# A recurrent mixer: loads and stores without the empty rows

## The chip, the cores and the metric

One Trainium2 chip, one core. The time is device microseconds of one execution; lower is better. Before the change three runs took 681.67, 686.21 and 689.05 us (median 686.21).

## The reference

Three stages, each over 4 batches and 768 time steps. First a recurrence in 8 heads of 40 x 40 state:

```python
for t in range(S):
    y[:, :, t] = einsum('bhd,bhde->bhe', rt, state)
    Sa = einsum('bhde,bhe->bhd', state, at)
    state = state * wt[:, :, None, :] - einsum('bhd,bhe->bhde', Sa, bt)
    state = state + einsum('bhd,bhe->bhde', vt, kt)
```

Then a gated convolution (five taps, a sigmoid, two 320 x 320 products) and a gated feed-forward part (320 to 1024, relu squared, back to 320, times a sigmoid gate). All values are float32.

## The kernel before

The recurrence is done in 24 chunks of 32 steps. A chunk's 32 pairs of batch and head lie as two halves of 16: 40 rows of the head dimension on partitions 0 to 39 for the even heads and 40 on partitions 64 to 103 (for v and r: 72 to 111) for the odd ones. The rows between the halves are empty; they hold zeros, or ones in w's columns.

For each chunk `plan_prep` loads `d` (w with its running product, then k, b and a; `load`, two transfers: columns 0 to 529 and the other 1536), runs a backward scan over w into `tl` (`bwd`, L181) and a forward scan into `ya` (`fwd`, L194), multiplies a by the forward scan (`ah`, L201) and k and b by the backward scan (`kbm`, L211), stores `ya` to DRAM (`yaout`), forms the small products of a with k and b (`gram`, L223, masked by `gmask`, L227) and transposes k and b (`ztr`, L236). `d`, `ya` are double-buffered. `plan_inv` inverts triangular 32 x 32 blocks on VectorE (L266, L267) for four chunks at a time. `plan_step` then does the recurrence between chunks: it loads v and r (`load_vr` into `vrt`), scanned rows from DRAM (`load_ys` into `ysj`, `load_wa` into `wa`) and multiplies v with r (`rv`, L359), the state with r (`yi`, L373) and so on (`gmm` L388, `umm` L400, `fmm` L420), ending with a new state. In `vrt` r stands in pairs of 32 columns, one of each pair zero in each half of the partitions, so that one matmul gives both halves' products side by side.

The two feed-forward stages (`Moe`) run beside this in 12 units of 64 steps. Their weights are split into two float32r parts on VectorE and ScalarE at the start (L683 to L699); L769, L821 and L829 are their matmuls.

All DMAs are issued by SyncE (SP) through `dma`, in one order. The order of all work is written out by hand: `ORDER` lists the tasks' numbers, and each engine and SP's queue get their instructions in that order. `BANKS` lists, in order of first use, which of four PSUM banks of its group a task's result goes to. A task that takes a bank waits until the bank's former user has been read. The numbers given to `add` beside an engine's letter (bytes and times of a DMA) do not reach the program.

Of the kernel before, what the change touches and what calls it, by code (L numbers as in the profile page):

```python
# [44 lines left out]
def mof(gr, i):  # L45
    return (i // 4) * 8 + gr * 4 + i % 4
# [49 lines left out]
class Attn:  # L96
    def __init__(self, ctx, tc, plan, fd, vr, vt, xs):
# [5 lines left out]
        psp = ctx.enter_context(tc.tile_pool(name="aps", bufs=1, space=PSUM))  # L103
        T = lambda name, shape: cp.tile(shape, F32, name=name)
        self.d = [T(f"d{i}", [PX, FDW]) for i in range(2)]
        self.ident = T("ident", [128, 128])
        make_identity(nc, self.ident)
        self.mask = T("mask", [128, L])
# [28 lines left out]
        self.s0 = [T(f"s0{i}", [PR, 8, D]) for i in range(2)]  # L137
        self.gs = [T(f"gs{i}", [128, 288]) for i in range(2)]
        self.ysj = T("ysj", [PX, NM, L + 1])
        self.ysb = T("ysb", [104, NM, 2 * L])  # L140
        self.vrt = [T(f"vrt{i}", [PR, 3 * NM * L]) for i in range(1)]
        self.tr = T("tr", [128, WCH, 8, L])
        self.sg, self.sz = T("sg", [128, WCH, 512]), T("sz", [128, 1, 640])
        self.pa = [psp.tile([128, 512], F32, name=f"pa{i}") for i in range(4)]
# [26 lines left out]

    def load(self, c, sl):
        self.dma(self.d[c % 2][:, sl], self.fd[c][:, sl])

    def kb(self, c):
        return self.d[c % 2][:, WL:WL + 1024]
# [34 lines left out]
        e.tensor_mul(kb, kb, t3.unsqueeze(2).to_broadcast([PX, 8, 2, L]))  # L211

    def yaout(self, c):
        self.dma(self.slya[c][0:PX], self.ya[c % 2])

    def gram(self, c, h):
        kb = self.kb(c).rearrange("p (m x) -> p m x", x=2 * L)
# [116 lines left out]
                 self.slz[c].rearrange("(x a) y -> a x y", x=2))  # L334

    def load_ys(self, c):
        self.dma(self.ysj.rearrange("p m l -> p (m l)"), self.slya[c][0:PX, 0:YS])

    def load_vr(self, c):
        self.dma(self.vrt[0], self.vr[c])  # L340

    def vpair(self, c, m):
        return self.vrt[0][:, m * L:m * L + L]

    def rpair(self, c, m):
        return self.vrt[0][:, NM * L + 2 * m * L:NM * L + 2 * m * L + 2 * L]

    def load_vt(self, c, gr):
        self.dma(self.mt[gr][64:96, :, 0:40], self.vt[c, gr])
# [5 lines left out]
    def rv(self, c):  # L355
        ps = self.bank("rv", c)
        for i in range(16):
            m, q, o = mof(i // 8, i % 8), i % 4, 2 * L * (i // 4)
            self.nc.tensor.matmul(ps[32 * q:32 * q + 32, o:o + 2 * L], lhsT=self.vpair(c, m), rhs=self.rpair(c, m),  # L359
                                  start=True, stop=True)  # L360

    def rvc(self, c):
# [6 lines left out]
    def yi(self, c, gr):  # L369
        s0, ps = self.s0[gr], self.bank("yi", c, gr)  # L370
        for i in range(8):
            r, o = i % 2 * 64, i // 2 * 2 * L
            self.nc.tensor.matmul(ps[r:r + 40, o:o + 2 * L], lhsT=s0[:, i, :], rhs=self.rpair(c, mof(gr, i)),  # L373
                                  start=True, stop=True)

    def yic(self, c, gr):
# [80 lines left out]
    def plan_prep(self, c):  # L457
# [3 lines left out]
        grams = [("gram", c - 2, h) for h in range(2)]  # L461
        add(("ldw", c), "d", [(1, 16, 7, 2120, 370)], lambda: self.load(c, slice(0, WL)),
            [("bwd", c - 2), ("fwd", c - 2)], p - 0.6)
        add(("ldk", c), "d", [(1, 16, 7, 6144, 370)], lambda: self.load(c, slice(WL, FDW)),
            grams + [("ah", c - 2)] + [("ztr", c - 2, k) for k in range(2)], p - 0.5)
        add(("bwd", c), "v", 1430, lambda: self.bwd(c),
            [("ldw", c), ("kbm", c - 1, 0), ("kbm", c - 1, 1), ("clc", c - 1), ("fwd", c - 1)], p)
# [5 lines left out]
        e = "v" if c < 3 else "g"  # L473
        for h in range(2):
            add(("kbm", c, h), e, 600 if e == "v" else 1250, lambda h=h: self.kbm(c, h, e), [("bwd", c), ("ldk", c)], p + 0.04)
        add(("yaout", c), "d", [(1, 16, 7, 4160, 380)], lambda: self.yaout(c), [("ah", c)], p + 0.3)
        for h in range(2):
            add(("gram", c, h), "p", 780, lambda h=h: self.gram(c, h),
                [("ah", c), ("kbm", c, h)], p + 0.1, bank=("a", "gram", c))
# [57 lines left out]
    def plan_step(self, c):  # L537
        P, add = self.plan, self.plan.add
        b = c + (HASTE[c] if c < len(HASTE) else 0.0)
        fs = lambda cc, g: [("fmm", cc, g, h) for h in range(2)]  # L540
        add(("lvr", c), "d", [(1, 16, 7, 6144, 370)], lambda: self.load_vr(c),
            [("rv", c - 1)] + [("yi", c - 1, g) for g in range(2)], b - 0.9)
        add(("lwa", c), "d", [(1, 10, 8, 2048, 370), (1, 16, 4, 2048, 370)], lambda: self.load_wa(c),
            [("yaout", c), ("stout", c, 0), ("gmm", c - 2, 0), ("gmm", c - 2, 1), ("fill", c % 2)], b - 0.8)
        add(("lzt", c), "d", [(1, 16, 8, 2560, 640)], lambda: self.load_zt(c),
            [("stout", c, 1), ("fill", 2 + c % 2)] + fs(c - 2, 0) + fs(c - 2, 1), b - 0.4)
        add(("lys", c), "d", [(1, 16, 7, 2112, 370)], lambda: self.load_ys(c),
            [("yaout", c)] + [("yb", c - 1, g, h) for g in range(2) for h in range(2)], b - 0.2)
        add(("rv", c), "p", 600, lambda: self.rv(c), [("lvr", c)], b - 0.1, bank=("a", "rv", c))
        add(("rvc", c), "a", 1520, lambda: self.rvc(c), [("rv", c)] + fs(c - 1, 0) + fs(c - 1, 1), b - 0.1,  # L550
# [408 lines left out]
def kernel(ctx, tc, fd, vr, vt, w_val, cw, w_out, mu, w_k, w_v, w_r, out, xs=None):  # L959
# [141 lines left out]
]  # L1101
BANKS = [
    "0123012301032201130320213031303230232231121313123100320122331231213220101230023102133111032203022303222121320132",
    "1023231231213012123123030232102103302101200313230203123130210310203321013202123012012032011032031203123010132101",
    "2301203123012313210123320122310031321202302203312031132003221332131223132313220210132103221032101220301202131232",
    "0310230303032011202302132130231033223132310230301123013231021323012012313030212330213101223012132323233223101221",
    "0323010321110320230321210211320301302112302132300231011301233120031213010120313122031130231031032313011023201130",
    "32232210321030231332013201",
]

# [1 line left out]
def arrays_of(inputs):  # L1112
    import numpy as np

    f = {k: np.ascontiguousarray(inputs[k]) for k in "rkvwab"}

    def fm(x):
        x = x.reshape(B, 4, 2, NCH, L, D).transpose(3, 2, 5, 1, 0, 4)
        return np.ascontiguousarray(x).reshape(NCH, 2, D, NM, L)

    def tm(x):
        x = x.reshape(B, 2, 2, 2, NCH, L, D).transpose(4, 5, 2, 1, 0, 3, 6)
        return np.ascontiguousarray(x.transpose(0, 2, 1, 3, 4, 5, 6)).reshape(NCH, 2, L, NM, D)
# [12 lines left out]
    fd = np.zeros((NCH, 128, FDW), np.float32)  # L1136
    f2 = fd.reshape(NCH, 2, 64, FDW)
    w = np.ones((NCH, 2, 64, NM, L + 1), np.float32)
    w[:, :, 0:D, :, 1:] = fm(f["w"])
    w[..., 0] = 0.0  # L1140
    f2[..., 0:YS] = w.reshape(NCH, 2, 64, YS)
    f2[:, :, 0:D, WL:WL + 1024] = np.stack([fm(f["k"]), fm(f["b"])], 4).reshape(NCH, 2, D, 1024)
    f2[:, :, 0:D, WL + 1024:] = fm(f["a"]).reshape(NCH, 2, D, 512)
    fd = np.ascontiguousarray(fd[:, 0:PX])
    vr = np.zeros((NCH, PR, 3 * NM * L), np.float32)
    r = np.zeros((NCH, PR, NM, 2, L), np.float32)
    for par in range(2):
        z = slice(72 * par, 72 * par + D)
        vr[:, z, 0:NM * L] = fm(f["v"])[:, par].reshape(NCH, D, NM * L)
        r[:, z, :, par] = fm(f["r"])[:, par]  # L1150
    vr[..., NM * L:] = r.reshape(NCH, PR, 2 * NM * L)
# [35 lines left out]
```

## Time and profile before

| | us or share |
|---|---|
| median of 3 runs | 686.21 |
| the profiled execution | 682.32 |
| its span | 680.3 |
| PE busy (matmuls) | 574.2, 84% |
| DVE busy | 525.3, 77% |
| ACT busy | 451.2, 66% |
| POOL busy | 236.9, 35% |
| SP's DMA queue | 116.75 MB, 66.2% of 16 DMA engines |

The busy times are averages over stages with different limits, so they are read by stretch, with the waits of each engine beside them. PE is TensorE, DVE VectorE, ACT ScalarE, POOL GpSimd; SPq is SyncE's queue, which issues the DMAs. L with a number is a line of the kernel. An engine's idle time counts only if somebody waits for that engine next.

### The profile page before, as it was taken

The page shows a single profiled execution, that of the slowest core. Times are in us where ns is not written, and L with a number is a line of the kernel's source. Part 1 is how long each engine was busy: PE and PEld are TensorE (multiplying, and loading weights), DVE is VectorE, ACT ScalarE, POOL GpSimd, SP SyncE. Part 2 cuts the span into 40 slices and gives each one's busy share as a digit, 9 for nine tenths or more (in the row PEclk, how much of TensorE's full clock was granted, in tenths as well). Part 3 has the DMA queues.
Part 4 walks back from the last instruction along what each step waited for, and adds up shares of the span by engine and source line. Part 5 has one row for each costly group of instructions (what it writes and reads, how often), then busy time and mean ns, then how long its engine had stood idle before and what let it go on. Part 6 is the DMA issues. An engine that isn't in the chain of part 4 may idle for free.

```text
span 680.3 us, 28916 instructions
## 1 busy us (share of the span) xinstructions
PE 574.2 (84%) x12368; PEld 519.3 (76%) x12368; DVE 525.3 (77%) x1236; ACT 451.2 (66%) x1153; POOL 236.9 (35%) x291
## 2 busy tenths in 40 slices
PE   2534367677889999999999898989999999999997
PEld 2433356566779978899888787979998989899897
DVE  9899878898878898889898876765898645545632
ACT  5545255355756767777686585768866889785843
POOL 1233223245153623446344423333313224151410
PEclk9999998566979999999999898999999999999999
DMA  8988989988877568876878835667527576332001
GB/s 250 266 266 280 256 232 225 267 217 260 218 196 161 170 196 227 250 158 180 273 202 137 206 87 149 166 167 148 150 68 163 132 176 171 83 84 74 1 20 40
DMA packets 137616, 118.59 MB, mean 174 GB/s; under 512 B 104208, under 2 KB 107280, under 8 KB 137488
## 3 DMA queue, kind: packets, MB, share of 16 engines
q1 hardware_dynamic: 137488, 116.75, 66.2%
q8 instruction: 97, 1.59, 1.1%
q14 instruction: 31, 0.25, 0.1%
HBM read 81.42 MB, written 35.30 MB: 172 GB/s over the span
## 4 chain that ended last, share of the span: by engine, by line
PE 59%; DVE 16%; ACT 7%; issue 6%; DMA 6%; POOL 1%; SPq 0%; DVEq 0%; POOLq 0%; ACTq 0%
PE pm L769 20%; PE pm L829 10%; PE pa L420 7%; PE pa L400 4%; PE pa L388 4%; PE pm L821 3%; PE pa L443 3%; PE pa L223 3%; PE pa L373 2%; DVE pm L949 2%; DMA d<-in_fd_dram 2%; PE pa L236 2%; DVE mt L429 2%; DVE tmv L266 2%; DVE tn L267 2%
## 5 line engine op out<-in xcount | busy, mean ns | idle before, releaser
L412 POOL TENSOR_TENSOR mt<-mt,mask 64x512 f32<-64x512 f32 x48 | 65.5, 1367 | 207.1 <-ACT mt L407 184.6
L407 ACT COPY mt<-pa 32x288 f32<-32x288 f32 x192 | 74.7, 389 | 16.3 <-PE pa L400 13.7
L769 PE MATMUL pm<-hh,whk 128*128 128x256 f32 x288 | 82.8, 296 | 1.4 <-ACT hh L739 0.9
L769 PE MATMUL pm<-hh,wlk 128*128 128x256 f32 x288 | 79.6, 285 | 0.0
L949 DVE SCALAR_TENSOR_TENSOR pm<-X,cw,pm 128x256 f32<-128x256 f32 (+1 forms) x144 | 67.0, 482 | 13.3 <-ACT pm L947 10.8
L420 PE MATMUL pa<-mt,zt 128*40 128x72 f32 x1536 | 63.5, 239 | 11.6 <-issue 5.2
L267 DVE TENSOR_TENSOR tn<-tn,tmv 128x31 f32<-128x31 f32 (+15 forms) x155 | 66.2, 427 | 5.3
L266 DVE TENSOR_TENSOR tmv<-tn,al 128x31 f32<-128x31 f32 (+15 forms) x155 | 62.9, 406 | 8.0 <-POOL tn L261 3.7
L420 PEld LDWEIGHTS pa<-mt,zt 128*40 128x40 f32 x1536 | 54.6, 124 | 18.5 <-issue 8.0
L429 DVE TENSOR_TENSOR mt<-pa,cl 40x160 f32<-40x160 f32 x184 | 58.5, 318 | 10.4 <-PE pa L420 8.5
L211 POOL TENSOR_TENSOR d<-d,tl 112x512 f32<-112x512 f32 x42 | 51.5, 1237 | 38.9 <-DVE tl L181 16.1
L829 PE MATMUL pm<-whv,kh 128*128 128x320 f32 x192 | 62.7, 326 | 0.0
L223 PE MATMUL pa<-ya,d 40*32 40x32 f32 x3072 | 42.8, 216 | 23.5 <-issue 10.5
L223 PEld LDWEIGHTS pa<-ya,d 40*32 40x32 f32 x3072 | 37.6, 128 | 30.3 <-issue 14.8
L829 PE MATMUL pm<-wlv,kh 128*128 128x320 f32 x192 | 59.5, 310 | 1.3 <-issue 1.3
L829 PE MATMUL pm<-whv,kl 128*128 128x320 f32 x192 | 59.5, 310 | 0.0
L769 PEld LDWEIGHTS pm<-hh,whk 128*128 128x128 f32 x288 | 55.6, 193 | 4.1 <-ACT hh L739 1.0
L236 PE MATMUL pa<-ident,d 104*128 104x104 f32 x192 | 35.8, 331 | 24.8 <-DVE d L211 11.8
L769 PEld LDWEIGHTS pm<-hh,wlk 128*128 128x128 f32 x288 | 55.7, 193 | 0.0
L769 PE MATMUL pm<-hl,whk 128*128 128x256 f32 x192 | 55.2, 288 | 0.4 <-POOL hl L744 0.4
L814 DVE TENSOR_TENSOR kl<-pm,kh 128x512 fp32r<-128x512 f32 x48 | 32.4, 686 | 28.1 <-ACT kh L812 27.9
L236 PEld LDWEIGHTS pa<-ident,d 104*128 104x128 f32 x192 | 25.3, 182 | 30.0 <-issue 11.0
(138 smaller groups left out, 1606.8 us busy)
## 6 DMA issues: line engine op xcount, KB each, us to landing
d<-in_fd_dram SPq DMA_DIRECT2D x24, 672.0 KB
vrt<-in_vr_dram SPq DMA_DIRECT2D x24, 672.0 KB
slya<-ya SPq DMA_DIRECT2D x24, 455.0 KB
slz<-sz SPq DMA_DIRECT2D x24, 320.0 KB
zt<-slz SPq DMA_DIRECT2D x24, 320.0 KB
d<-in_fd_dram SPq DMA_DIRECT2D x24, 231.9 KB
ysj<-slya SPq DMA_DIRECT2D x24, 231.0 KB
slg<-sg SPq DMA_DIRECT2D x20, 256.0 KB
```

Source lines behind the costliest of these rows:

```text
L211: e.tensor_mul(kb, kb, t3.unsqueeze(2).to_broadcast([PX, 8, 2, L]))
L223: self.nc.tensor.matmul(ps[p:p + L, m * L:(m + 1) * L], lhsT=kb[r:r + 40, m, o:o + L], rhs=ah[r:r + 40, m, :], start=True, stop=True)
L236: self.nc.tensor.transpose(ps[:, 128 * i:128 * i + 104], self.kb(c)[0:104, o:o + 128], self.ident[0:104, 0:104])
L266: v.tensor_mul(t3, tn[:, 0:h, k:k + 1].to_broadcast([128, h, nt]), al[:, k:k + 1, k + 1:n].to_broadcast([128, h, nt]))
L267: v.tensor_add(tn[:, 0:h, k + 1:n], tn[:, 0:h, k + 1:n], t3)
L407: self.nc.scalar.copy(self.mv(gr)[96:128, 4 * mh:4 * mh + 4, par, :], ps[32 * q:32 * q + 32, 0:288].rearrange("p (m x) -> p m x", x=72))
L412: self.nc.gpsimd.tensor_mul(mm, mm, self.mask[64:128].unsqueeze(1).to_broadcast([64, 16, L]))
L420: self.nc.tensor.matmul(ps[r:r + 40, k * 72:k * 72 + 72], lhsT=self.zt[c % 2][:, zof(mof(gr, i)) + par, :], rhs=self.mt[gr][:, 2 * i + par ...
L429: self.nc.vector.tensor_mul(self.mv(gr)[0:40, 4 * mh:4 * mh + 4, par, 0:40], p3[r:r + 40, :, 0:40], cn[r:r + 40, m0:m0 + 4].unsqueeze(2).t ...
L769: self.nc.tensor.matmul(ps[0:n, (mt % 2) * NT:(mt % 2) * NT + NT], lhsT=ww[:, mt * 128:mt * 128 + n], rhs=xx, start=(i == 0), stop=(i == l ...
L829: self.nc.tensor.matmul(ps[:, 0:DM], lhsT=xx[:, k, sl], rhs=ww, start=(k == 0 and i == 0), stop=(k == 7 and i == 2))
L949: self.nc.vector.scalar_tensor_tensor(o, X[0:n, k, :, t:t + TW], self.cw[0:n, k, t:t + 1], o, ALU.mult, ALU.add)
```

## The change

The rows between the halves are no longer moved. k, b and a are loaded in two transfers of 48 rows (partitions 0 to 47 and 64 to 111) in place of one of 112; w's columns are loaded as before. The scanned rows are stored and loaded back in two times 48 rows. v and r are packed anew: `vrt` is three layers of 16 x 32 columns, and each half of the partitions gets two layers (r and v on partitions 0 to 47 in layers 0 and 1; v and r on partitions 64 to 111 in layers 1 and 2), so that the zero partner of r in each half is a layer that no transfer writes. r's pair of 32 columns is then layer 0 and layer 2, two runs of 32 columns. What no transfer writes is filled with zeros once at the start: `d` on VectorE, `ysj` and `vrt` on GpSimd. `ORDER` is unchanged; `BANKS` names other banks in some places, 168 of 586. The figures in `add` change, and the host packs v and r anew.

```diff
         self.d = [T(f"d{i}", [PX, FDW]) for i in range(2)]
+        for t in self.d:
+            nc.vector.memset(t[32:64, WL:], 0.0)
...
         self.ysj = T("ysj", [PX, NM, L + 1])
+        nc.gpsimd.memset(self.ysj[32:64], 0.0)
...
-        self.vrt = [T(f"vrt{i}", [PR, 3 * NM * L]) for i in range(1)]
+        self.vrt = T("vrt", [PR, 3, NM, L])
+        nc.gpsimd.memset(self.vrt, 0.0)
...
+    def load_k(self, c):
+        for r in (0, 64):
+            self.dma(self.d[c % 2][r:r + 48, WL:], self.fd[c][r:r + 48, WL:])
...
     def yaout(self, c):
-        self.dma(self.slya[c][0:PX], self.ya[c % 2])
+        for r in (0, 64):
+            self.dma(self.slya[c][r:r + 48], self.ya[c % 2][r:r + 48])
...
     def load_ys(self, c):
-        self.dma(self.ysj.rearrange("p m l -> p (m l)"), self.slya[c][0:PX, 0:YS])
+        for r in (0, 64):
+            self.dma(self.ysj[r:r + 48].rearrange("p m l -> p (m l)"), self.slya[c][r:r + 48, 0:YS])
 
     def load_vr(self, c):
-        self.dma(self.vrt[0], self.vr[c])
+        for i in range(2):
+            self.dma(self.vrt[64 * i:64 * i + 48, i:i + 2].rearrange("p z m l -> p (z m l)"), self.vr[c, i])
 
     def vpair(self, c, m):
-        return self.vrt[0][:, m * L:m * L + L]
+        return self.vrt[:, 1, m]
 
     def rpair(self, c, m):
-        return self.vrt[0][:, NM * L + 2 * m * L:NM * L + 2 * m * L + 2 * L]
+        return self.vrt[:, 0:3:2, m]
...
-            self.nc.tensor.matmul(ps[32 * q:32 * q + 32, o:o + 2 * L], lhsT=self.vpair(c, m), rhs=self.rpair(c, m),
+            self.nc.tensor.matmul(self.two(ps[32 * q:32 * q + 32, o:o + 2 * L]), lhsT=self.vpair(c, m), rhs=self.rpair(c, m),
                                   start=True, stop=True)
...
-        add(("ldk", c), "d", [(1, 16, 7, 6144, 370)], lambda: self.load(c, slice(WL, FDW)),
+        add(("ldk", c), "d", [(2, 16, 3, 6144, 370)], lambda: self.load_k(c),
...
 BANKS = [
-    "0123012301032201130320213031303230232231121313123100320122331231213220101230023102133111032203022303222121320132",
+    "0123012301032201130320213031303230232231121313123100320122331231213220101232003120133111230003200323002121302130",
```

VectorE's first instructions of before, from the start of the program (`rst`, `seed`, `xj` are constants, `pa` the PSUM banks, `tl` the first backward scan):

```order
L118 MEMSET rst 112x530
L119 MEMSET rst 112x17
L122 MEMSET seed 112x528
L129 MEMSET xj 128x256
L146 MEMSET pa_130 128x512
L146 MEMSET pa_131 128x512
L146 MEMSET pa_132 128x512
L146 MEMSET pa_133 128x512
L848 MEMSET X 128x12x4
L181 SCALAR_TENSOR_TENSOR tl<-d_68,rst 112x529
```

The same of the changed kernel:

```order
L107 MEMSET d_68 32x1536
L107 MEMSET d_69 32x1536
L120 MEMSET rst 112x530
L121 MEMSET rst 112x17
L124 MEMSET seed 112x528
L131 MEMSET xj 128x256
L150 MEMSET pa_134 128x512
L150 MEMSET pa_135 128x512
L150 MEMSET pa_136 128x512
L150 MEMSET pa_137 128x512
L863 MEMSET X 128x12x4
L189 SCALAR_TENSOR_TENSOR tl<-d_68,rst 112x529
```

The two fills of `d` stand ahead of all that was there.

SP's first DMAs of before, with what each waits for (DMAHW0 to DMAHW7 are eight counters that the DMAs use in turn; DVE, PE and so on are engines):

```order
L156 DMA d_68<-in_fd_dram 112x530
L643 DMA buf<-in_cw_dram 128x30
L156 DMA d_68<-in_fd_dram 112x1536
L156 DMA d_69<-in_fd_dram 112x530
L643 DMA wt<-in_w_val_dram 64x640 x2
L156 DMA mt<-in_vt_dram 32x16x40
L643 DMA buf<-in_w_val_dram 128x640
L643 DMA wt<-in_w_val_dram 128x640 [waits DMAHW0_49]
L643 DMA mu<-in_mu_dram 128x6 [waits DMAHW1_49]
L156 DMA d_69<-in_fd_dram 112x1536 [waits DMAHW2_49]
L156 DMA slya_186<-ya_104 112x1040 [waits DMAHW3_49,DVE_49]
```

The same of the changed kernel:

```order
L160 DMA d_68<-in_fd_dram 112x530
L658 DMA buf<-in_cw_dram 128x30
L160 DMA d_68<-in_fd_dram 48x1536 [waits DVE_49]
L160 DMA d_68<-in_fd_dram 48x1536
L160 DMA d_69<-in_fd_dram 112x530
L658 DMA wt<-in_w_val_dram 64x640 x2
L160 DMA mt<-in_vt_dram 32x16x40
L658 DMA buf<-in_w_val_dram 128x640 [waits DMAHW0_49]
L658 DMA wt<-in_w_val_dram 128x640 [waits DMAHW1_49]
L658 DMA mu<-in_mu_dram 128x6 [waits DMAHW2_49]
L160 DMA d_69<-in_fd_dram 48x1536 [waits DMAHW3_49,DVE_49]
L160 DMA d_69<-in_fd_dram 48x1536 [waits DMAHW4_49]
```

The k load of the first chunk is a pair, and the first of the pair waits for VectorE's fill; from the ninth DMA on each waits for the eighth before it, which with the pairs is a later piece of work than it was.

## Rows read from the trace of the kernel before

**Rows 1.** Busy us by stretch: span, each engine (instructions), PEclk, DMA share, GB/s

```profile
0.00:60.00 60.00, 22.59 (x857) 19.08 (x858) 56.05 (x111) 31.71 (x71) 14.71 (x24) 1.00 0.93 272
60.00:120.00 60.00, 34.93 (x1206) 29.48 (x1209) 50.66 (x121) 27.90 (x79) 18.36 (x16) 0.95 0.93 234
120.00:200.00 80.00, 59.97 (x1524) 51.73 (x1513) 71.12 (x166) 43.96 (x116) 30.64 (x30) 0.67 0.87 239
200.00:440.00 240.00, 226.61 (x4852) 204.63 (x4851) 201.03 (x474) 169.78 (x440) 103.04 (x122) 0.99 0.71 181
440.00:681.00 241.00, 230.07 (x3953) 214.36 (x3951) 146.40 (x368) 177.87 (x449) 70.13 (x99) 1.00 0.44 107
```

**Rows 2.** DVE's waits, 0 to 200 us: releaser, us in total, times, longest

```profile
DVE pm L689 <- DMA buf<-in_w_v_dram: 1.6, 2, 1.2
DVE tmv L266 <- DMA al<-slg: 1.2, 1, 1.2
...
DVE pm L689 <- DMA buf<-in_w_out_dram: 0.6, 1, 0.6
...
DVE tl L181 <- DMA d<-in_fd_dram: 0.4, 1, 0.4
```

**Rows 3.** Waits of POOL and PE that DMAs ended, whole trace

```profile
POOL d L211 <- DMA d<-in_fd_dram: 15.5, 4, 9.7
...
PE pa L359 <- DMA vrt<-in_vr_dram: 0.3, 1, 0.3
```

**Rows 4.** SP's DMA queue (packets, MB, share) and issues (KB each)

```profile
q1 hardware_dynamic: 137488, 116.75, 66.2%
...
d<-in_fd_dram SPq DMA_DIRECT2D x24, 672.0 KB
vrt<-in_vr_dram SPq DMA_DIRECT2D x24, 672.0 KB
```

**Rows 5.** DVE's timeline at the start: start us, us, line, operation

```profile
0.98 0.50 DVE L118 MEMSET rst<- 112x530 f32 x1 [0.98 <-PEq L1174]
...
2.56 2.11 DVE L146 MEMSET pa<- 128x512 f32 x4
4.64 1.22 DVE L181 TENSOR_TENSOR_SCAN tl<-d,rst 112x529 f32<-112x529 f32 x1
```

**Rows 6.** DVE's timeline at 18 us, the idle time before in brackets

```profile
18.07 1.26 DVE L181 TENSOR_TENSOR_SCAN tl<-d,rst 112x529 f32<-112x529 f32 x1 [0.82 <-ACT cl L190]
```

**Rows 7.** POOL's timeline at the start

```profile
2.62 0.95 POOL L260 MEMSET tn<- 128x1024 f32 x1
...
21.31 1.47 POOL L201 TENSOR_TENSOR ya<-d,ya 112x512 f32<-112x512 f32 x1 [17.53 <-DVE ya L194]
```

**Rows 8.** SP's issues by tile: ns min/median/max, first and last start

```profile
L156 SPq DMA_DIRECT2D d<-in_fd_dram x48: 312/408/2520, 0.8 to 411.6; - x48
...
L156 SPq DMA_DIRECT2D vrt<-in_vr_dram x24: 322/424/1717, 33.8 to 594.5; - x24
...
L156 SPq DMA_DIRECT2D slya<-ya x24: 303/380/1637, 9.3 to 439.2; - x24
...
L156 SPq DMA_DIRECT2D ysj<-slya x24: 304/549/2416, 51.2 to 612.9; - x24
```

**Rows 9.** SP's waits: us in total, times, longest

```profile
SPq L156 <- PE pa L420: 49.1, 18, 11.1
...
SPq L156 <- DMA d<-in_fd_dram: 10.2, 9, 2.7
```

**Rows 10.** PE's groups by form: out<-in, shapes, count, busy us, mean ns

```profile
L373 PE MATMUL pa<-vrt,s 112*40 112x64 f32 x736 | 28.8, 226 | 2.0 <-ACT s L446 1.9
L359 PE MATMUL pa<-vrt 112*32 112x64 f32 x768 | 16.9, 227 | 4.5 <-issue 2.7 <-DVE ysb L436 0.6 <-ACT s L446 0.5
```

**Rows 11.** Timelines of DVE and PE at 117 us

```profile
117.18 0.68 DVE L227 TENSOR_TENSOR sg<-pa,gm 128x512 f32<-128x512 f32 x1
...
117.37 1.18 PE L373 MATMUL pa<-vrt,s 112*40 112x64 f32 x16
```

More of the change, by code (lines that the diff above doesn't have):

```diff
@@ L336, in load_ys, with two @@
     def load_ys(self, c):
-        self.dma(self.ysj.rearrange("p m l -> p (m l)"), self.slya[c][0:PX, 0:YS])
+        for r in (0, 64):
+            self.dma(self.ysj[r:r + 48].rearrange("p m l -> p (m l)"), self.slya[c][r:r + 48, 0:YS])
     def load_vr(self, c):
-        self.dma(self.vrt[0], self.vr[c])
+        for i in range(2):
+            self.dma(self.vrt[64 * i:64 * i + 48, i:i + 2].rearrange("p z m l -> p (z m l)"), self.vr[c, i])
     def vpair(self, c, m):
-        return self.vrt[0][:, m * L:m * L + L]
+        return self.vrt[:, 1, m]
     def rpair(self, c, m):
-        return self.vrt[0][:, NM * L + 2 * m * L:NM * L + 2 * m * L + 2 * L]
+        return self.vrt[:, 0:3:2, m]
+    @staticmethod
+    def two(ps):
+        return ps.rearrange("p (r l) -> p r l", l=L)
     def load_vt(self, c, gr):
@@ L372, in yi @@
             r, o = i % 2 * 64, i // 2 * 2 * L
-            self.nc.tensor.matmul(ps[r:r + 40, o:o + 2 * L], lhsT=s0[:, i, :], rhs=self.rpair(c, mof(gr, i)),
+            self.nc.tensor.matmul(self.two(ps[r:r + 40, o:o + 2 * L]), lhsT=s0[:, i, :], rhs=self.rpair(c, mof(gr, i)),
                                   start=True, stop=True)
@@ L475, in plan_prep @@
             add(("kbm", c, h), e, 600 if e == "v" else 1250, lambda h=h: self.kbm(c, h, e), [("bwd", c), ("ldk", c)], p + 0.04)
-        add(("yaout", c), "d", [(1, 16, 7, 4160, 380)], lambda: self.yaout(c), [("ah", c)], p + 0.3)
+        add(("yaout", c), "d", [(2, 16, 3, 4160, 380)], lambda: self.yaout(c), [("ah", c)], p + 0.3)
         for h in range(2):
@@ L540, in plan_step @@
         fs = lambda cc, g: [("fmm", cc, g, h) for h in range(2)]
-        add(("lvr", c), "d", [(1, 16, 7, 6144, 370)], lambda: self.load_vr(c),
+        add(("lvr", c), "d", [(2, 16, 3, 4096, 370)], lambda: self.load_vr(c),
             [("rv", c - 1)] + [("yi", c - 1, g) for g in range(2)], b - 0.9)
@@ L546, in plan_step @@
             [("stout", c, 1), ("fill", 2 + c % 2)] + fs(c - 2, 0) + fs(c - 2, 1), b - 0.4)
-        add(("lys", c), "d", [(1, 16, 7, 2112, 370)], lambda: self.load_ys(c),
+        add(("lys", c), "d", [(2, 16, 3, 2112, 370)], lambda: self.load_ys(c),
             [("yaout", c)] + [("yb", c - 1, g, h) for g in range(2) for h in range(2)], b - 0.2)
@@ L1102 @@
 BANKS = [
-    "0123012301032201130320213031303230232231121313123100320122331231213220101230023102133111032203022303222121320132",
[L1104 to L1107, printed above, removed]
+    "0123012301032201130320213031303230232231121313123100320122331231213220101232003120133111230003200323002121302130",
+    "1023031031013010123103230230120103320101220313030023123132012310023301213022103210210230211030231023103210130101",
+    "0321003123210313010123302120312031301020320203310231130203021330131203130313022012130123021230121202301022131032",
+    "2310032323030211022300130132031033203130310232301103213031221303210210313032012332013101203210130303033203121201",
+    "2303012301112320032301012011302301320110320132302031211321233100231013210102313120231132031231232313211023021130",
     "32232210321030231332013201",
@@ L1144, in arrays_of @@
     fd = np.ascontiguousarray(fd[:, 0:PX])
-    vr = np.zeros((NCH, PR, 3 * NM * L), np.float32)
-    r = np.zeros((NCH, PR, NM, 2, L), np.float32)
+    vr = np.zeros((NCH, 2, 48, 2 * NM * L), np.float32)
     for par in range(2):
[L1148 to L1151, printed above, removed]
+        z = slice(8 * par, 8 * par + D)
+        vr[:, par, z, NM * L * (1 - par):NM * L * (2 - par)] = fm(f["v"])[:, par].reshape(NCH, D, NM * L)
+        vr[:, par, z, NM * L * par:NM * L * (par + 1)] = fm(f["r"])[:, par].reshape(NCH, D, NM * L)
     a = {"fd": fd, "vr": vr,
```

## The prediction, made before the changed kernel ran

> **What bounds the kernel now.** I read the busy time by stretch first [rows 1]. There are two kernels in one. Up to 200 us VectorE (DVE) is busy 56.05 of 60, 50.66 of 60 and 71.12 of 80 us, together 177.8 of 200; TensorE (PE) is busy 117.5. From 200 us to the end PE is busy 456.7 of 481 us, and DVE falls to 347. The DMA engines are nearly full early (0.93, 0.93, 0.87) and have room later (0.71, 0.44). So a full DMA share and a full DVE stand side by side in the first 200 us, and the question is which of them the other waits for. For that I read who ended DVE's waits in the first 200 us [rows 2]: DMA rows add up to 1.6 + 1.2 + 0.6 + 0.4 = 3.8 us, of which only the 0.4 us belongs to a tile that the change touches (the scan's wait on d, and that on its unchanged columns). The 15.5 us that POOL waited on loads of d in the whole trace [rows 3] are idle time of an engine that is busy only 33.1 of the first 120 us [rows 1]. So DVE paces the early part and PE the late part; the loads arrive mostly in time.
>
> **The change part by part.**
>
> Bytes. For each of 24 chunks the k/b/a load goes from 112 to 96 rows of 6144 B (98,304 B less), the scanned rows' store from 112 to 96 rows of 4160 B (66,560 B), their load back from 112 to 96 of 2112 B (33,792 B), and v with r from 112 x 6144 B to 96 x 4096 B (294,912 B). The two largest sizes of before are in [rows 4]. That is 493,568 B a chunk, 11.85 MB in all, 10.1% of the queue's 116.75 MB. The queue's packets took 66.2% of 680.3 us, so about 45 us of time of all 16 DMA engines goes. What that is worth is set by the waits that DMAs end, not by the 45 us. On DVE up to 200 us these are 3.8 us [rows 2]; a tenth fewer bytes takes at least a tenth of them, 0.4 us, and at most all, 3.8 us. A nearly full queue gets shorter by more than its bytes, so I take half: **-1.9 us** (bounds -0.4 and -3.8). After 200 us PE has 24.3 us of idle time in 481 us [rows 1]; PE's own wait on v and r is 0.3 us in the whole trace [rows 3], so I add nothing there.
>
> Two new zero fills on DVE. They are the first instructions of its program, 32 x 1536 each. The trace has DVE fills of 112 x 530 in 0.50 us and of 128 x 512, four in 2.11 us [rows 5], 0.94 to 1.03 ns for a column. 1536 columns are 1.45 to 1.58 us, two of them 2.9 us. In before, DVE ran from 0.98 to 4.67 us through such fills and started the first scan without a wait, at 4.64 [rows 5]; the load of w for it had landed. So the whole 2.9 us goes ahead of the first scan, and everything that DVE does in the first 60 us (idle there 3.95 us, 0.98 of it before its first instruction) stands behind it. The first cover is the scan at 18.07 us, which waited 0.82 us for ACT's copy of the totals [rows 6]: ACT is not moved by the fills up to that point, so 0.8 us is absorbed. **+2.1 us** is left (bounds 0 and +2.9: nothing if later waits swallow it all). The first k load also waits now for the fill of d0, at about 0.98 + 1.45 = 2.4 us where it was issued at 1.72 before; k and b are multiplied only after both first scans, which end later by the same 2.9 us, so this is covered.
>
> Two new zero fills on POOL, 112 x 1536 and 32 x 528. POOL's fill of 128 x 1024 took 0.95 us [rows 7], so these are about 1.4 and 0.5 us. Behind them POOL has nothing that anyone wants soon: it sat idle 17.5 us until 21.31 [rows 7]. **0.**
>
> Split transfers. Each of the four becomes two issues, 96 more on SP's one queue. The medians of an issue are 408 ns (d), 424 (vrt), 380 (slya) and 549 (ysj) [rows 8]; 24 x (0.408 + 0.424 + 0.380 + 0.549) = 42 us of SP time. What hides it is that SP waits for others: for PE L420 alone 49.1 us [rows 9]. The second half matters only where a load ends somebody's wait on the path, and then by one issue, 0.4 us, against a transfer that is shorter. Of DVE's and PE's waits above, none or one is of that kind. **+0.3 us** (bounds 0 and +42). The order also shows that every DMA waits for the eighth one before it (the names DMAHW0 to 7 go round). With pairs the eighth one before is a more recent one; SP's waits that ended with a landing of d were 10.2 us in 9 cases [rows 9]. While the queue is full its engines have work anyway, so I count this at 0, and keep it as a rival.
>
> [...] First the row: a second issue costs 0.38 to 0.55 us of SP, and the rows beside it show no price for the transfer itself being cut in two. [...]
>
> Matmuls with v and r. Their moving operand, 112 x 64 before in one run, is now two runs of 32 with a gap. Nothing in this trace has that form. 736 matmuls of the state with r fill 28.8 us, 768 of v with r 16.9 us [rows 10]. If the two runs cost nothing, 0; if each such matmul took twice its share, +45.7 us. The nearest rows are these same matmuls, with as many columns and rows, and only the place of half of the columns differs; I take **0**.
>
> PSUM banks. 168 of the 586 bank uses get another bank; the order of work is the same. I followed both strings through the program and, for each use, asked in the trace of before whether the bank's previous user was done when the use begins. With the new string this fails once: the state-times-r matmuls at 117.37 now take the bank that DVE L227 reads until 117.18 + 0.68 = 117.86 [rows 11]. **+0.5 us** (bounds 0 and +3, since ends and starts move).
>
> The sum: 2.1 - 1.9 + 0.3 + 0.5 = **+1.0 us**. The profiled execution took 682.3 us (680.3 of span and 2.0 around it), so its like would take 683.3. That execution is near the lowest of the three timed runs (681.67, 686.21, 689.05); against their median of 686.21 I forecast **687.2 us**, no change that can be measured: a difference under 1%, 6.9 us, can't be told from none here.
>
> **The rivals.**
>
> DMA paces the early part after all. For it: shares of 0.93, 0.93 and 0.87 mean 181 us of work of all engines in the first 200 us [rows 1]. Then 10.1% of that, 18 us, goes, and with the fills 2.1 us come back: 686.2 - 18 + 2.1, about 670 us. Against it: 3.8 us of DVE waits. Half of this gain, 678 us, is where it would first be told from nothing.
>
> The queue of issues becomes the bound (slower). Place: SP, in the stretches where it issues one DMA right after another. Price: the step's two loads, v with r and the scanned rows, each 24 times, 24 x (0.424 + 0.549) = 23 us, giving about 710 us; with all four, 42 us and 728. It decides from the point where SP has the next issue ready and nothing to wait for; 17 of the 96 extra issues on the path are 6.9 us. Against it: SP's waits for engines [rows 9]. [...]
>
> The two-run operand costs (slower). At twice the share 686 + 45.7, 732 us; even a sixth more would pass 1%. Nothing in the trace speaks for it.
>
> [...]
>
> **How the numbers follow.** No change, as summed: 0.57, with a range of its own from 680 to 693. DMA paces: 0.18. Issues bound: 0.12. Two-run operand: 0.04. Clock: 0.09, split about evenly, 0.04 faster and 0.05 slower. So faster by over 1% 0.22, within 1% 0.57, slower by over 1% 0.21. For 8 in 10 the range must take in the nearer halves of the rivals on both sides: from 675 (beyond it the better half of the DMA case, 0.09) to 699 (beyond it most of the issue case and the operand, about 0.11).
>
> **What would show it.** Right: DVE's first scan at about 7.5 us in place of 4.64 and the scan of 18.07 at about 20.2; about 105 MB on the queue and a DMA share of about 0.6; PE's matmuls of v and r at a mean of 226 ns as before; PE busy about 457 us after 200 us, and DVE about as busy as before in the first 200. Wrong: DVE work that ends well before 200 us while DVE's idle time there falls by more than 4 us (the DMA case); SP's waits that end with a landing much over 10 us, and waits of PE or POOL on vrt or ysj (the issue case); longer rows for v and r (the operand); another clock in 100 to 200 us.

## The result, and the profile after

The changed kernel takes 673.21 us (median of 4 runs, 672.54 to 675.11) against 685.46 (4 runs, 681.67 to 689.05): a ratio of 0.985 with a 95% interval from 0.981 to 0.990. It is 1.5% faster, 14 us below the forecast of 687.2 and just below the forecast's range (675 to 699). The ratios here and below leave out executions in a slower state of the chip, the medians do not, so the two can differ by some tenths of a percent.

Busy time by stretch of the changed kernel (columns as in [rows 1], the last stretch ends with the span of 671.2 us):

```profile
0.00:60.00 60.00, 22.76 (x869) 19.22 (x872) 57.39 (x111) 31.00 (x70) 17.36 (x26) 1.00 0.92 243
60.00:120.00 60.00, 36.45 (x1158) 30.75 (x1152) 50.89 (x122) 28.16 (x79) 18.33 (x16) 1.00 0.94 225
120.00:200.00 80.00, 59.92 (x1565) 51.83 (x1564) 69.03 (x161) 44.33 (x118) 30.62 (x30) 0.96 0.82 202
200.00:440.00 240.00, 229.39 (x5164) 208.15 (x5163) 212.09 (x502) 177.45 (x459) 107.29 (x126) 1.00 0.73 172
440.00:672.00 232.00, 222.12 (x3632) 206.95 (x3630) 139.99 (x347) 170.55 (x430) 67.21 (x96) 1.00 0.39 92
```

DVE's busy time in the first 200 us is 57.39 + 50.89 + 69.03 = 177.3 us, against 177.8 in [rows 1]: DVE gained nothing there, and the DMA share is still 0.92, 0.94 and 0.82. Most of the difference lies behind 200 us: between 200 and 440 us DVE does 212.09 us of work instead of 201.03 and PE 229.39 instead of 226.61. PE's idle time from 200 us to the end of the span is 471.2 - 451.5 = 19.7 us, against 480.3 - 456.7 = 23.6. That is 3.9 of the 9.1 us between the two spans. The rest is PE's work: 119.1 us of it lie before 200 us instead of 117.5, and in all it is busy 570.7 us instead of 574.2.

The chain of work that ended last (followed back from the last instruction; shares of the span by engine), before and then after:

```profile
PE 59%; DVE 16%; ACT 7%; issue 6%; DMA 6%; POOL 1%; SPq 0%; DVEq 0%; POOLq 0%; ACTq 0%
```

```profile
PE 63%; DVE 14%; ACT 8%; issue 6%; DMA 3%; SPq 1%; POOL 1%; DVEq 0%; ACTq 0%; POOLq 0%
```

In the kernel before, 6% of the span on this chain is time of DMAs. Added up by its pieces it is 37.7 us, 26.1 of them up to 200 us and 11.6 between 200 and 440; in the changed kernel it is 22.7 us. The prediction did not use this row; it counted the 3.8 us of DVE's direct waits alone.

SP's queue, and the four split transfers (columns as in [rows 4]):

```profile
q1 hardware_dynamic: 137488, 104.91, 64.8%
...
d<-in_fd_dram SPq DMA_DIRECT2D x48, 288.0 KB
slya<-ya SPq DMA_DIRECT2D x48, 195.0 KB
vrt<-in_vr_dram SPq DMA_DIRECT2D x48, 192.0 KB
...
ysj<-slya SPq DMA_DIRECT2D x48, 99.0 KB
```

The bytes fell as worked out, by 10.1%. The time of the packets did not: 64.8% of 671.2 us is 434.9 us of all 16 engines, against 66.2% of 680.3 us, 450.4, in [rows 4]. That is only 3.4% less, and the share of about 0.6 that the prediction named as a sign of being right did not come. The number of packets is the same by chance: 1,536 packets of data are gone, and the 96 added transfers brought 1,536 packets of 4 bytes. A tenth fewer bytes takes nearly as long, so a byte became dearer. This line is the first sight of what the prediction had missed.

DVE's start in the changed kernel (a timeline: start us, us, line, operation; answers to [rows 5, 6]):

```profile
1.19 1.34 DVE L107 MEMSET d<- 32x1536 f32 x1 [1.19 <-PEq L1187]
2.79 1.34 DVE L107 MEMSET d<- 32x1536 f32 x1 [0.27 <-issue]
...
7.96 1.22 DVE L189 TENSOR_TENSOR_SCAN tl<-d,rst 112x529 f32<-112x529 f32 x1
...
20.26 1.25 DVE L189 TENSOR_TENSOR_SCAN tl<-d,rst 112x529 f32<-112x529 f32 x1
```

The two fills and their gaps put the first scan at 7.96 instead of 4.64, and the scan of 18.07 at 20.26.

The matmuls with v and r by form (answers to [rows 10]), and waits that DMAs ended (us in total, times, longest; answer to [rows 3, 9]):

```profile
L388 PE MATMUL pa<-vrt,s 112*40 112x64 f32 x736 | 29.6, 230 | 1.9 <-ACT s L461 1.7
L374 PE MATMUL pa<-vrt 112*32 112x64 f32 x768 | 17.0, 234 | 1.4 <-ACT s L461 0.5 <-DVE ysb L451 0.5 <-DVE sg L236 0.4
```

```profile
POOL ya L209 <- DMA ysj<-slya: 16.4, 1, 16.4
...
POOL d L219 <- DMA d<-in_fd_dram: 3.1, 1, 3.1
...
PEld pa L374 <- DMA vrt<-in_vr_dram: 0.2, 1, 0.2
```

```profile
SPq L160 <- DMA d<-in_fd_dram: 11.7, 16, 1.5
```

The operand costs next to nothing (230 and 234 ns, against 226 and 227 in [rows 10]). POOL's waits for d look shorter than the 15.5 us of [rows 3], but its idle time is still there and is put down to another releaser. A wait of POOL that ends with a load of ysj was named as a sign of the issue case; this one is an old wait, too:

```profile
63.02 2.04 POOL L219 TENSOR_TENSOR d<-d,tl 112x512 f32<-112x512 f32 x1 [9.69 <-PE pa L245]
...
125.61 1.17 POOL L209 TENSOR_TENSOR ya<-d,ya 112x512 f32<-112x512 f32 x1 [16.43 <-DMA ysj<-slya]
```

In the kernel before, the same two pieces of work start at 62.16 and 124.49 us, after idle times of 9.65 (put down to a load of d) and 15.98 us (to a load of weights). SP is not held up more either: its waits that a landing of d ended are 11.7 us against 10.2.

Where on the time axis the two profiled executions part, by the start of the same piece of work in each trace (scan is the backward scan, L181 in before; state is the first matmul of the step at L388 in before; the differences are worked out from the starts):

```
work (before)       starts at   after minus before
scan of chunk 0        4.6        +3.3
scan of chunk 4       32.9        +0.8
scan of chunk 15     197.1        +3.4
state of chunk 4     208.3        -0.7
state of chunk 10    350.9        -2.9
state of chunk 12    390.4        -6.7
state of chunk 15    462.1        -9.8
state of chunk 23    609.8        -9.2
```

Until 197 us the changed kernel is behind, as forecast. In this pair of executions it gains between 197 and 460 us. One of the places, around 375 us, shows how a late transfer reaches PE. First the kernel before, in timelines of SP, POOL, DVE, ACT and PE (idle time ahead of a row and its releaser in brackets):

```profile
356.80 7.88 SPq L156 DMA_DIRECT2D al<-slg  x4
...
368.14 1.32 SPq L156 DMA_DIRECT2D td<-tn  x2
```

```profile
374.39 0.95 POOL L260 MEMSET tn<- 128x1024 f32 x1 [3.10 <-DMA td<-tn]
```

```profile
375.59 0.19 DVE L266 TENSOR_TENSOR tmv<-tn,al 128x31 f32<-128x31 f32 x1 [1.98 <-POOL tn L261]
```

```profile
380.45 0.41 ACT L739 CAST hh<-f 128x256 fp32r<-128x256 f32 x1 [1.96 <-DVE f L801]
```

```profile
381.24 0.70 PE L420 MATMUL pa<-mt,zt 128*40 128x72 f32 x16 [2.25 <-ACT sz L240]
```

Then the same in the changed kernel:

```profile
354.58 4.42 SPq L160 DMA_DIRECT2D al<-slg  x4
...
363.14 1.32 SPq L160 DMA_DIRECT2D td<-tn  x2
```

```profile
368.98 0.95 POOL L269 MEMSET tn<- 128x1024 f32 x1 [0.65 <-DMA td<-tn]
```

```profile
370.63 1.01 DVE L275 TENSOR_TENSOR tmv<-tn,al 128x31 f32<-128x31 f32 x1
```

```profile
376.21 0.70 PE L435 MATMUL pa<-mt,zt 128*40 128x72 f32 x16 [0.17 <-ACT sz L249]
```

In before, SP took 7.88 us to get four small loads out, and the stores of tn went out behind them. POOL, which must clear tn, waited 3.10 us for one of the stores, DVE 1.98 for POOL, ACT 1.96 for DVE and PE 2.25 for ACT. In the changed kernel the four loads took 4.42 us and PE's wait is 0.17; PE's start there is 5.0 us ahead of before, where 12 us earlier it was 3.0 ahead, so the place is worth 2.1 us. The chain that ended last runs through the store in the kernel before, and through no DMA here in the changed one:

```profile
368.84 5.41 DMA td<-tn
```

None of the transfers in this chain is one that the change touches, and PE's wait is put down to ACT, three steps from the DMA. A count of the waits that DMAs end directly, as in [rows 2, 3], does not see such a loss at PE. That the four loads made the store late is not shown: the profile's chain comes to SP's stores from PE (L443).

### The profile page after: what moved, and what is told of

The parts are those of the page before. It is cut to its first block, busy times and chain, and to the rows that moved or that the text cites. A ratio compares the mean times of both kernels' runs of the same rounds, so it can differ in the third digit from the quotient of the medians.

```text
span 671.2 us, 29098 instructions
## 1 busy us (share of the span) xinstructions
PE 570.6 (85%) x12368; PEld 516.9 (77%) x12368; DVE 529.4 (79%) x1238; ACT 451.5 (67%) x1153; POOL 240.8 (36%) x293
## 3 DMA queue, kind: packets, MB, share of 16 engines
q1 hardware_dynamic: 137488, 104.91, 64.8%
## 4 chain that ended last, share of the span: by engine, by line
PE 63%; DVE 14%; ACT 8%; issue 6%; DMA 3%; SPq 1%; POOL 1%; DVEq 0%; ACTq 0%; POOLq 0%
PE pm L784 20%; PE pm L844 11%; PE pa L435 7%; PE pa L415 4%; PE pa L403 4%; PE pa L232 3%; PE pm L836 3%; PE pa L388 3%; PE pa L458 3%; DVE pm L964 2%; DMA d<-in_fd_dram 2%; PE pa L245 2%; DVE mt L444 2%; PE pa L374 2%; DVE tmv L275 1%
## 5 line engine op out<-in xcount | busy, mean ns | idle before, releaser
L784 PE MATMUL pm<-hh,whk 128*128 128x256 f32 x288 | 81.3, 292 | 1.6 <-ACT hh L754 0.9
L784 PE MATMUL pm<-hh,wlk 128*128 128x256 f32 x288 | 78.2, 281 | 0.0
L219 POOL TENSOR_TENSOR d<-d,tl 112x512 f32<-112x512 f32 x42 | 53.4, 1283 | 36.6 <-PE pa L245 12.6
L844 PE MATMUL pm<-whv,kh 128*128 128x320 f32 x192 | 62.6, 326 | 1.7 <-issue 1.7
L784 PEld LDWEIGHTS pm<-hh,whk 128*128 128x128 f32 x288 | 54.2, 188 | 4.3 <-ACT hh L754 1.1
L784 PEld LDWEIGHTS pm<-hh,wlk 128*128 128x128 f32 x288 | 54.3, 188 | 0.0
```

The lines of the kernel that those rows point to most:

```text
L784: self.nc.tensor.matmul(ps[0:n, (mt % 2) * NT:(mt % 2) * NT + NT], lhsT=ww[:, mt * 128:mt * 128 + n], rhs=xx, start=(i == 0), stop=(i == l ...
L844: self.nc.tensor.matmul(ps[:, 0:DM], lhsT=xx[:, k, sl], rhs=ww, start=(k == 0 and i == 0), stop=(k == 7 and i == 2))
```

## The experiments

Before each ratio stands the median; the ratio is to the kernel before on the same chip, with its 95% interval. "DMA time" is the queue's share times the span of the profiled execution (450.4 us before, 434.9 after); the mean time of a packet is taken from the packets of the trace (6144 bytes: 352 ns before, 435 after, where only k, b and a still have this size).

**The bytes.** The first group keeps the changed kernel and gives bytes back. The first of them gives back all: rows 48 to 63, and all three layers of v and r, so that it differs from the changed kernel in what moves (and in how the host lays out v and r) and in nothing else.

```
+FULL_EARLY, FULL_LATE = True, True
...
+        return ((0, 64), (64, 112)) if (FULL_EARLY if c < at else FULL_LATE) else ((0, 48), (64, 112))
...
-        for r in (0, 64):
-            self.dma(self.d[c % 2][r:r + 48, WL:], ...)
+        for r, e in self.halves(c, 16):            # ya, ysj and v/r in the same way
+            self.dma(self.d[c % 2][r:e, WL:], ...)
```

> The changed kernel with all the bytes back: each pair of transfers carries rows 0 to 63 and 64 to 111, and v and r come with all three layers, so 112 rows move as before, in twice the number of transfers; fills, banks and the two-run operand are those of the changed kernel. Theory A (fewer bytes shorten waits that DMAs end, most of them after 200 us, where TensorE has no slack): the gain goes, 685 us or more, up to 690 with the fills. Theory B (only the start and the banks shift the work, so TensorE meets fewer stretches at the low clock; bytes don't matter): 671 to 676 as the changed kernel. Theory C (the new banks take waits away): 671 to 676 as well.

Measured: 697.17 us, 1.016 (1.009 to 1.023), above all three expectations. It is slower than the kernel before, with the same bytes:

```profile
q1 hardware_dynamic: 139024, 116.75, 69.9%
```

69.9% of 695.4 us is 486 us of DMA time, where before took 450.4 for the same 116.75 MB. So two things of size stand against each other in the change: the split form with all bytes costs about 1.6%, and the missing bytes give back 0.9852 / 1.016, that is 3%, some 21 us (the two intervals leave 15 to 27).

The next two save the bytes in one part of the chunks only (k, b, a, ya, ysj from chunk 16 on or up to chunk 15; v and r from chunk 5 on or up to 4), which parts the transfers at about 200 us but for 0.4 MB of ysj (chunks 5 to 15), counted as early:

```
+FULL_EARLY, FULL_LATE = True, False        # the other: False, True
```

> As e_full, but the bytes are saved for the late part alone: k loads, stores and reloads of scanned rows from chunk 16 on, v and r from chunk 5 on, which is what was issued after about 200 us; the early part moves all rows. 7.2 of the 11.85 MB stay saved. Theory A (what counts is saved after 200 us): 673 to 677. A rival of it (DMA paces the first 200 us after all): 682 to 687. Theories B and C: 671 to 676.

Measured: 682.11 us, 1.000 (0.996 to 1.004).

> The mirror: bytes saved for the early part alone (k and scanned rows of chunks 0 to 15, v and r of chunks 0 to 4; 4.65 of 11.85 MB), all rows moved later. Theory A (late savings count): 682 to 687. Its rival (DMA paces the first 200 us): 673 to 677. Theories B and C: 671 to 676.

Measured: 684.25 us, 1.000 (0.996 to 1.004). Against 1.016 with no byte saved, the 7.2 MB that are saved late and the 4.65 MB that are saved early are worth 1.6% each (about 0.8% either way), 11 us, and both together 3%. So neither part of the program is free of the transfers. The theory that only the late waits count falls as well as the prediction's that only the early ones do.

Does more saving go on paying? Here v and r are loaded for the first chunk only:

```
-        for i in range(2):
+        for i in range(2 if c == 0 else 0):
             self.dma(self.vrt[64 * i:64 * i + 48, i:i + 2]...
```

> The changed kernel with v and r loaded for the first chunk only and used again for the other 23: 9.0 MB fewer and 46 transfers fewer, so its output is that of other data. It asks whether fewer bytes go on paying. If the DMA engines pace the kernel all along at some 2 us for a megabyte: 653 to 660 us. If the gain ends where TensorE and VectorE bound it by their own work (TensorE was busy 451.5 of 471 us after 200 us in the changed kernel): 666 to 673 us.

Measured: 671.25 us, 0.983 (0.976 to 0.990), which can't be told from the changed kernel's 0.985.

```profile
q1 hardware_dynamic: 134544, 95.86, 57.8%
```

```profile
200.00:440.00 240.00, 229.99 (x5152) 208.31 (x5153) 211.42 (x497) 176.61 (x458) 106.68 (x125) 0.99 0.63 151
```

9 MB less, a DMA share of 0.63 instead of 0.73 in this stretch, and PE's 229.99 us and DVE's 211.42 are those of the changed kernel. At the 3% for 11.85 MB from above, 9 MB would have been worth over 2%; the intervals leave at most about 1%. So most of the gain has run out: PE is busy 230 of 240 us in this stretch with either amount of bytes.

**The split.** The kernel before, with its four transfers cut in two and nothing else changed: no bytes saved, no fills, the old operand, the old banks. Once the cut is between rows, at row 64, and once it takes even and odd rows.

```
+CUT = [slice(0, 64), slice(64, 112)]       # the other: [slice(0, 112, 2), slice(1, 112, 2)]
-        self.dma(self.vrt[0], self.vr[c])
+        for r in CUT:                               # d, ya and ysj in the same way
+            self.dma(self.vrt[0][r], self.vr[c][r])
```

> The kernel before with its four transfers of d (k, b, a), ya, ysj and v/r each cut at row 64 into two (rows 0 to 63 and 64 to 111): the same bytes, 96 transfers more, no fills, the old operand, the old banks. It asks what made the kernel with all bytes back (697.2 us) 14.5 us slower than the kernel before (682.65). Theory halves (a transfer that stays on half the rows is served more slowly: in the kernel with all bytes back a packet of 6144 bytes took 407 ns against 352): 692 to 700 us, packets of 6144 bytes at about 405 ns. Theory count (96 more issues and counters on SP's queue): 692 to 700 us as well, with packets of 6144 bytes near 352 ns and SP's own issue time as the reason. Theory structure (fills and the operand in two runs): 681 to 685 us.

Measured: 693.44 us, 1.011 (1.005 to 1.017).

> The same as the cut at row 64, but each of the four transfers is cut into its even and its odd rows: the same bytes, the same 96 transfers more, yet each spreads over all rows from 0 to 111. Theory halves: the packets of 6144 bytes go back towards 352 ns and the time to that of the kernel before, 681 to 686 us. Theory count: as slow as the cut at row 64, 692 to 700 us. Theory structure: 681 to 685 us, as the other cut.

Measured: 685.16 us, 0.997 (0.993 to 1.002). The queue and the first three stretches of the cut at row 64:

```profile
q1 hardware_dynamic: 139024, 116.75, 70.9%
```

```profile
0.00:60.00 60.00, 22.78 (x856) 19.20 (x857) 55.58 (x109) 31.51 (x71) 14.67 (x24) 1.00 0.99 266
60.00:120.00 60.00, 35.59 (x1156) 30.16 (x1155) 49.03 (x120) 26.63 (x75) 17.41 (x16) 1.00 0.99 235
120.00:200.00 80.00, 58.08 (x1546) 49.82 (x1543) 66.04 (x154) 42.86 (x116) 28.70 (x29) 0.96 0.91 222
```

And of the cut into even and odd rows:

```profile
q1 hardware_dynamic: 138640, 116.75, 65.8%
```

```profile
0.00:60.00 60.00, 22.44 (x855) 18.94 (x856) 53.87 (x107) 29.68 (x65) 14.74 (x24) 1.00 0.89 259
60.00:120.00 60.00, 35.24 (x1151) 29.76 (x1145) 52.30 (x124) 29.08 (x82) 18.48 (x16) 1.00 0.93 246
120.00:200.00 80.00, 61.55 (x1576) 53.27 (x1576) 67.69 (x161) 44.84 (x119) 31.02 (x30) 0.96 0.82 223
```

Both have 96 transfers more than before. In the even-and-odd kernel SP's issues take 430 us in all, where they took 321 in before (summed over the trace). Where each half keeps to its rows, the DMA share goes to 0.99, 0.99 and 0.91, the DMA time to 489 us, and a packet of 6144 bytes takes 419 ns. Where each half spreads over all rows, the share is 0.89, 0.93 and 0.82, the DMA time 450 us, the packet takes 348 ns, and the time is that of the kernel before. So 96 issues and their counters cost nothing that can be measured (0.997), and with transfers that keep to one half of the rows a packet took a fifth longer than with transfers over all rows (419 ns against 348). This is most of the cost of the split form (1.1 of 1.6%), and it comes with which rows a transfer reaches. The rows are rows of SBUF and of DRAM at once, and the even-and-odd kernel has 384 fewer packets of 4 bytes; none of these was varied by itself.

**One part of the change alone**, each put into the kernel before with the old banks. First v and r (packed loads, GpSimd's fill, the operand in two runs), then the rows of k, b, a, ya and ysj with their fills:

```
+        for i in range(2):
+            self.dma(self.vrt[64 * i:64 * i + 48, i:i + 2]..., self.vr[c, i])
```

> The kernel before with only the part on v and r: two packed loads of 192 KB in place of one of 672 KB, the buffer filled once by GpSimd, the operand in two runs; 7.1 MB fewer, 24 transfers more, the old banks. At 24 us for 11.85 MB (from the kernel with all bytes back against the changed one) 7.1 MB are worth -14 us, and a quarter to a third of the split's 14.5 us comes against it: 671 to 675 us, most of the whole change. If the operand in two runs held the 14.5 us instead: 680 to 685 us.

Measured: 676.61 us, 0.986 (0.978 to 0.993).

```
+CUT = [slice(0, 48), slice(64, 112)]       # d (fills on VectorE), ya, ysj (fill on GpSimd)
```

> The kernel before with only the part on rows: k, b, a, ya and ysj in two transfers of 48 rows each, d's fills on VectorE, ysj's fill on GpSimd; 4.8 MB fewer, 72 transfers more, the old banks. 4.8 MB at 2 us each are worth -10 us, and two thirds to three quarters of the split's 14.5 us come against it (+10 to +11), with some 2 us of fills: 682 to 688 us, no gain. If the split costs nothing for these three (the structure of v and r held it): 672 to 676 us.

Measured: 679.80 us, 0.988 (0.981 to 0.996). Their queues:

```profile
q1 hardware_dynamic: 137488, 109.67, 63.0%
```

```profile
q1 hardware_dynamic: 137488, 111.98, 66.3%
```

The part on v and r brings nearly the whole gain by itself; its median is a little above the 671 to 675 us expected. The part on rows brings more than expected, though its DMA time (66.3% of 677.8 us, 449) is that of before, so the DMA time alone does not order the kernels. By their middles the two gains do not add up: 1.4% and 1.2% alone, 1.5% together. That would fit a gain that runs out, as in the run without v and r, but each has an interval of 0.8% either way, so it is not shown.

**Parts of the changed kernel undone or moved.** The old table of banks:

> The changed kernel with the banks of before. Theory C (banks take waits away): most of the 12 us comes back, 680 to 685. Theory A: 672 to 675, since only one bank use differs by about 0.5 us in the trace. Theory B: anything from 671 to 680, with the clock of the run.

Measured: 675.02 us, 0.989 (0.985 to 0.993), against 0.985 (0.981 to 0.990): no difference that can be told.

d's two fills on GpSimd:

```
-            nc.vector.memset(t[32:64, WL:], 0.0)
+            nc.gpsimd.memset(t[32:64, WL:], 0.0)
```

> The changed kernel with d's two zero fills on GpSimd in place of VectorE: nothing else moves. It prices the term that the forecast gave the fills (+2.1 us). In the profile of the changed kernel the first scan starts 3.3 us later than before, the scan of 18.07 us 2.2 us later, and from 33 us on what is left is 0.8 us. If the first scan's delay stays on the path: 670 to 671.5 us (673.2 less 2 to 3). If it is swallowed, as the 0.8 us at 33 us says: 672 to 674 us.

Measured: 673.32 us, 0.987 (0.983 to 0.990). The first scan starts at 4.64 again, and nothing that can be measured comes of it. The two intervals would hide some 4 us, so the run bounds the fills' cost and does not show it to be nothing.

k, b and a in one transfer of 112 rows again, without the fills:

```
-        for r in (0, 64):
-            self.dma(self.d[c % 2][r:r + 48, WL:], self.fd[c][r:r + 48, WL:])
+        self.dma(self.d[c % 2][:, WL:], self.fd[c][:, WL:])
```

> The changed kernel with k, b and a loaded as before (one transfer of all 112 rows, 672 KB, no fills), all else as changed: 2.4 MB more, 24 transfers fewer. Theory halves: dropping the rows of d costs as much as it saves, since packets of 6144 bytes take 435 ns on half the rows (2304 of them, 62.6 us of all 16 engines) and about 350 ns on all rows (2688, 59 us), and the fills go as well: 670 to 674 us, packets near 350 ns. Theory bytes alone (24 us for 11.85 MB): 2.4 MB more are 4.8 us more, 677 to 679 us.

Measured: 674.90 us, 0.990 (0.984 to 0.996), between the two expectations and not to be told from the changed kernel. Packets of 6144 bytes take 369 ns; 2688 of them are 61.9 us of all engines, 2304 at 435 ns in the changed kernel 62.6. For k, b and a, leaving a seventh of the rows out saves their packets no time at all.

The two halves of d side by side, the second issued by ScalarE on a queue of its own:

```
+            (self.nc.scalar if r else self.nc.sync).dma_start(self.d[c % 2][r:r + 48, WL:], ...)
```

> The changed kernel with the second half (rows 64 to 111) of each load of k, b, a issued by ScalarE on its own queue, so that both halves can move side by side: the same bytes and transfers. [...] If ScalarE waits there for the buffer of d, work behind it is late: 676 us or more, with idle time of ScalarE at that line. If the halves theory is wrong: packets stay at 435 ns.

Measured: 701.33 us, 1.028 (1.022 to 1.035). The two queues, then waits of POOL and SP:

```profile
q1 hardware_dynamic: 135952, 97.83, 57.1%
q10 hardware_dynamic: 1536, 7.08, 4.4%
```

```profile
POOL d L219 <- DMA d<-in_fd_dram: 40.1, 6, 14.3
```

```profile
SPq L160 <- DMA d<-in_fd_dram: 51.3, 18, 9.8
```

The packets did get faster (382 ns on SP's queue, 419 on ScalarE's, against 435), but the loads came late: POOL waited 40.1 us for d instead of 3.1, and SP's waits that a landing of d ended are 51.3 us instead of 11.7. ScalarE issued its half after SP's in 19 of 24 chunks, by up to 16.0 us: in this kernel the issue stands in ScalarE's own order of work. So this does not show what halves side by side would be worth with issues on time.

No kernel among these is faster than the changed one by more than the measurement can tell.

## Why the prediction was wrong, step by step

**Bytes (-1.9 us): mis-sized by ten.** The step that failed is "What that is worth is set by the waits that DMAs end", with the count of 3.8 us up to 200 us and nothing added after. Half of the 3.8 was the author's estimate; in the two profiled executions a tenth fewer bytes took only 3.4% off the DMA time. At equal form the bytes are worth 21 us, about half from either part of the program. The direct waits did not even shrink (DVE's rows ended by DMA up to 200 us are about 4 us in both kernels). DMAs stood for 6% of the chain that ended last in before, which would have been a wider bound than 3.8 us. One route was seen at 375 us, where PE's wait appears under ACT. It is worth some 2 us and does not carry the result: PE's wait at this place is 1.92 to 2.38 us in the four kernels that move all bytes and 0.17 in the changed one, but 1.84 in the kernel with d's fills on GpSimd, which takes the changed kernel's time. Nor does SP's time for the four loads go with the bytes; the kernel with even and odd rows, and then the one with k, b and a in one transfer:

```profile
363.37 3.91 SPq L157 DMA_DIRECT2D al<-slg  x4
```

```profile
358.48 7.78 SPq L158 DMA_DIRECT2D al<-slg  x4
```

**Split transfers (+0.3 us): mis-sized, too, and for another reason than the one weighed.** The term was priced by issues of SP. Those cost nothing that can be measured, as forecast: the cut into even and odd rows has all 96 and loses nothing (0.997). But the cut at row 64 costs 1.1%, 7 us (9.3 by the medians), with slower packets (419 ns against 352 in before). The bounds of 0 and +42 us held that, though they were made of issues. The prediction's sentence that "the rows beside it show no price for the transfer itself being cut in two" was true, and nothing was then put in for such a price.

**The two errors had opposite signs**, and it is luck that the sum of +1.0 us missed by only 14: -21 for bytes, +7 for the halves, and the rest of the split form's price. That rest, 1.016 against 1.011 for the form with everything and the cut alone, lies within the two intervals and is not settled.

**Fills (+2.1 us): not told from 0.** The fills took 2 x 1.34 us and delayed the first two scans to 7.96 and 20.26, as written (about 7.5 and 20.2). But only 0.8 us of it is left at 33 us, and with the fills on GpSimd the time is the same within some 4 us. The prediction's other bound, that later waits swallow it all, fits better.

**Operand in two runs (0): right.** The means are 230 and 234 ns against 226 and 227 in [rows 10]; the kernel with the old operand and even and odd rows shows 230 and 233, so these few ns are not the operand's. **Banks (+0.5 us): not told from 0, nor from what was forecast.** **GpSimd's fills (0) and the eight counters (0): right**, the former by the trace (0.53 and 1.38 us, and POOL sat idle 17.81 us before its work at 23.49), the latter by the even and odd rows (0.997).

**The rivals.** "DMA paces the early part" named the right resource and a time (670 us) near the measured one, but not the course, so the time is luck: its 18 us of DMA work in the first 200 us did not go (181 us before, 177 after), at 197 us the changed kernel is still 3.4 us behind, and half of the bytes' worth is late. "The queue of issues" and "the operand" fell. **The clock** (0.09 of the chances): no run shows what a shift of work would be worth through it. In the profiled execution of before, the granted clock was 0.57 from 192 to 200 us where the changed kernel had 1.00, and part of the step from +3.4 to -0.7 us there may be this. It does not carry the result: the changed kernel's runs at a mean clock of 0.950 and 0.994 took 672.5 and 672.9 us. Nor does PE's busy time from 120 to 200 us go with it: it is 59.97 us for 1524 matmuls at 0.67 [rows 1] and 59.92 us for 1565 at 0.96, and the kernel with even and odd rows has 0.96 there and the time of before.

**What stays open**: through which waits the bytes pay, the early and the late ones. The kernel with even and odd rows has more DVE waits ended by DMA in the first 200 us than before (14 us against 4) and the same time, so this view does not sort the kernels. Neither does the share of DMAs in the chain that ended last: 6% before, 3% after, but 9% with even and odd rows and 7% without v and r, which take the times of before and after. Each kernel has one profiled execution.

## What to carry to other kernels

When bytes are taken out of a queue that is busy two thirds of the time, don't price them by the waits that its transfers end directly: a late transfer can reach the busy engine through three others (at 375 us PE waited 2.25 us for ACT, three steps from a store), and the share of DMAs in the chain that ended last is a wider bound to set beside those waits (6%, 37.7 us, against 3.8). The DMA time that goes is no safe bound: the part on rows alone gained 1.2% (0.4 to 1.9) with the DMA time of before. Ask of a new transfer which rows it reaches, not only how many bytes and issues it has: here, where a seventh of the rows left out meant one half at a time, the DMA time stayed what it was (449 us against 450), and nearly the whole gain came with the part that leaves out much more (v and r, 384 KB in place of 672; 0.986 against 0.985 for all). Then ask where the gain ends: past 1.5% another 9 MB bought nothing that could be measured (0.983 against 0.985).

## What the runs showed of the hardware

A packet of 6144 bytes took 348 ns on average in transfers over even or odd rows from 0 to 111, and 419 in transfers over rows 0 to 63 or 64 to 111, with the same bytes, number of transfers and order of work. In these two kernels that is 20% for a packet. What in the hardware makes the difference, no run here shows.

SP issued 96 transfers more in the same time: 685.16 us against 684.12, though its issues took 430 us in all instead of 321. Moving half of each load of k, b and a to ScalarE's queue, on the other hand, cost 28 us (701.33 against 673.21); that it did so by the loads coming late fits the trace (POOL waited 40.1 us for d instead of 3.1) but was not tried alone.
